# Hash bits as sign bits taken from PSUM, and sent by DMA instead of moved by VectorE

## The chip, the core and the metric

The kernel runs on one core of one Trainium2 chip. A core has five engines that run side by side, each with its own queue in order: TensorE (PE: matmul, with weight loads as PEld), VectorE (DVE), ScalarE (ACT), GpSimd (POOL) and SyncE (SP, which here only issues DMAs). Sixteen DMA engines move data between HBM and the on-chip memory (SBUF) and within SBUF. Matmul results land in PSUM, in tiles that pools share out. The metric is the device time of the whole kernel in microseconds.

## What is computed

Attention in which a query sees only keys of its own hash bucket, followed by a gated feed-forward block. Cut to what matters:

```python
# q, k, v: (4, 8, 768, 64); proj: (64, 6)
q_bits = (q @ proj > 0); k_bits = (k @ proj > 0)     # six bits each
mask = bucket(q_bits)[:, None] == bucket(k_bits)[None, :]
scores = where(mask, q @ k.T / 8, -1e9)
attn = softmax(scores); x = attn @ v                 # -> (3072, 512)
xn = x / sqrt(mean(x * x) + 1e-6) * rms_g
out = (silu(xn @ w_gate) * (xn @ w_val)) @ w_out
```

The kernel does not build the mask. It lays six more rows under the 64 rows of q and of k, one for each bit, each row +c or -c by the bit. The product of two matching bits is the same positive number, of two others its negative; where all six match the sum is 1536, and the exponential is taken with a bias of -192 after a scale of 1/8, so that any mismatch drops the weight to nearly nothing.

## The kernel before

**Tiling.** Four batches of eight heads; heads go in pairs (b, hp). A unit u is half of a batch's 768 queries (384) for all eight heads; there are eight units. Work is laid out in 192 steps. A step is a third of one head of one unit: two score matmuls of 128 keys by 384 queries (`scores`, L314) and one exponential over both (`probs`, L329). In each step the scores of the next step are issued first, then the exponential of this one, then a list of other work, `plan[t]`, filled by hand through `at(...)`. So each engine's order is fixed by the order in which the program issues; there is no scheduler behind it. The first two heads run for units 0 and 1 in turn, so the heads of pair 1 of batch 0 begin at step 12, of pair 2 at step 18, of pair 3 at step 24. The feed-forward block of a unit (`gate`, `value`, `project`) is spread over the steps of later units by `spread` (L692), which weighs pieces against a target per step; `inserts` holds pieces that are tied to a step (hash products, weight HASH, and sums of v, weight MEAN).

**Getting q and k.** A pair's q and k come from HBM as natural rows (batch 0 and the first two pairs of batch 1, `ONPE`) and are transposed on TensorE (`turn_pe`, L143); the PSUM result is copied into `qT` and `kT`, for batch 0's pairs 1 to 3 the k part by VectorE and the q part by ScalarE (L599 to L607). GpSimd casts them into the 16-bit tile `QK` (`cast_pool`). The other pairs come as 32 by 32 blocks and are transposed on VectorE (`turn_dve`). Values are cast by `v_prep`, on GpSimd but for pair 0.

**Hash bits.** `hash_direct` (L237), for ONPE pairs: small fp32 matmuls with proj give `d_ps` in PSUM, one group of 32 partitions for each of k and q of each head. VectorE makes signs (`signs`, L210: greater than 0, minus 0.5) into a tile `bits`. Then either VectorE copies six rows at a time to rows 64 to 69 of `QK` (`move`, L247: k scaled up to 512, q left at 0.5) or, for two pairs of batch 1, VectorE scales the whole tile by `own` and SP sends the rows by four DMAs (`send`, L257). In batch 0 all four pairs are moved by VectorE. `hash_one` (L268), for the ten other pairs: signs, then two multiplications by `sel` (`select`, L217) that blank the other head's bits, so that one DMA can write 12 rows for both heads; four DMAs per pair, and their score matmuls take 76 rows instead of 70.

**Queues.** SP issues in order the loads of q, k and v, the bits, and the stores of the output. In batch 0 its order is: loads of pair 3 of batch 0, values of pairs 2 and 3, then k, q and v of batch 1's pairs 0 and 1, then the block loads. Each of SP's DMAs uses one of eight semaphores and so waits for the landing of the eighth before it. GpSimd issues the feed-forward weights as casting DMAs: two halves of the gate weights (steps 3 and 7), two of the value weights (12 and 16), two of the output weights (39 and 42). All run on the same sixteen engines.

## Time and profile before

| | us |
|---|---|
| median of three runs | 341.23 (341.08 to 341.37) |
| profiled execution | 342.05 |
| its span | 340.3 |
| TensorE busy | 331.1 |
| VectorE busy | 249.0 |
| ScalarE busy | 226.7 |
| GpSimd busy | 152.9 |

Busy time is a sum over instructions; TensorE's matmuls overlap, so a busy TensorE is not one at its peak. A group of instructions is shown by its line in the code, engine, operation, result and source (partitions by elements), count, busy time, mean duration in ns, and idle time before it with what ended it. A stretch shows the busy time of each engine between two times. SP's rows are issues, and a row of several issues also holds the waits between them. When a DMA lands is told by the trace's DMA and semaphore records.

### The profile page before, as it was taken

Reading aid. Unit: us, or ns where it says so; the run is one execution under the profiler, and the core shown is the slowest. Engines: PE = TensorE matmul, PEld = TensorE weight load, DVE = VectorE, ACT = ScalarE, POOL = GpSimd, SP = SyncE. Lnnn points to the kernel's source line nnn. Section 1 sums busy time; section 2 is a strip of 40 time slices with the busy share of each in tenths; the row PEclk is TensorE's granted clock in tenths of the full one; section 3 lists DMA queues with packets and bytes.
Section 4 is the critical chain, followed back from the end, with each engine's and each line's share of the span. In section 5 each row is a group of like instructions: output and inputs, shape, how many; then the busy total and the mean of one; then the engine's idle time right before and its main releaser. Section 6 shows DMA issues by size and latency. Waiting matters only on the chain.

```text
span 340.3 us, 7757 instructions
## 1 busy us (share of the span) xinstructions
PE 331.1 (97%) x3004; PEld 198.0 (58%) x3004; DVE 249.0 (73%) x518; ACT 226.7 (67%) x331; POOL 152.9 (45%) x218
## 2 busy tenths in 40 slices
PE   8898999999999999999999999999999999999996
PEld 4465756655556555655656556555655656664554
DVE  3789996778889669977798758986796546674870
ACT  2889886666666767676667767776667767763322
POOL 4389939427553632746373523737280121112000
PEclk9999999999999999999999999999999999999999
DMA  7999965932728427251717017001100010001002
GB/s 222 291 213 272 236 119 91 173 103 46 165 49 158 91 94 144 35 115 64 133 55 139 7 68 157 24 3 41 64 7 4 1 64 33 0 2 64 31 0 92
DMA packets 79028, 31.20 MB, mean 92 GB/s; under 512 B 64928, under 2 KB 75024, under 8 KB 78992
## 3 DMA queue, kind: packets, MB, share of 16 engines
q1 hardware_dynamic: 75888, 25.73, 31.5%
q0 software_dynamic: 2656, 4.72, 8.0%
q8 instruction: 23, 0.38, 0.4%
q10 hardware_dynamic: 448, 0.27, 0.3%
q14 instruction: 13, 0.11, 0.1%
HBM read 28.32 MB, written 6.29 MB: 102 GB/s over the span
## 4 chain that ended last, share of the span: by engine, by line
PE 88%; DVE 7%; ACT 3%; issue 1%; DVEq 0%
PE g_ps L425 18%; PE v_ps L425 17%; PE y_ps L454 17%; PE s_ps L321 17%; PE o_ps L346 9%; PE d_ps L204 3%; PE x_ps L408 2%; DVE QK L251 2%; PE t_ps L150 2%; ACT psb L333 2%; PE d_ps L229 2%; DVE bits L212 1%; PE z_ps L525 1%; DVE a L442 1%; DVE kT L152 1%
## 5 line engine op out<-in xcount | busy, mean ns | idle before, releaser
L333 ACT ACTIVATE psb<-s_ps,ebias 128x768 f16<-128x768 f32 x192 | 168.3, 901 | 23.5 <-PE s_ps L321 22.7
L321 PE MATMUL s_ps<-QK 76*128 76x384 f16 (+1 forms) x384 | 93.8, 325 | 1.9 <-ACT psb L333 1.1
L433 ACT ACTIVATE t<-g_ps 128x384 f32<-128x384 f32 x96 | 47.2, 491 | 57.5 <-PE g_ps L425 57.3
L425 PE MATMUL g_ps<-xnT,wg 128*128 128x384 f16 x384 | 82.7, 325 | 0.4
L425 PE MATMUL v_ps<-xnT,wv 128*128 128x384 f16 x384 | 81.5, 325 | 0.7 <-DVE a L442 0.6
L442 DVE SCALAR_TENSOR_TENSOR a<-t,g_ps 128x384 f32<-128x384 f32 x96 | 52.8, 550 | 26.9 <-ACT t L433 25.3
L454 PE MATMUL y_ps<-wo,ht 128*128 128x512 f16 x276 | 68.0, 378 | 0.2 <-ACT ysb L466 0.2
L367 POOL TENSOR_TENSOR x<-otmp,rcp 128x384 f32<-128x384 f32 x31 | 25.7, 830 | 89.9 <-DVE rcp L365 89.4
L346 PEld LDWEIGHTS <-psb 128*128 128x128 f16 x1152 | 51.7, 97 | 19.6 <-issue 3.4
L443 DVE SCALAR_TENSOR_TENSOR ht<-a,v_ps 128x384 f16<-128x384 f32 x96 | 53.2, 554 | 11.1 <-PE v_ps L425 2.7
L346 PE MATMUL o_ps<-vl,psb 128*128 128x65 f16 x1152 | 56.4, 193 | 1.4 <-DVE otmp L360 1.4
L321 PEld LDWEIGHTS <-QK 76*128 76x128 f16 (+1 forms) x384 | 34.9, 98 | 35.1 <-issue 10.1
L425 PEld LDWEIGHTS <-wv 128*128 128x128 f16 x384 | 35.3, 97 | 23.3 <-issue 2.5
L425 PEld LDWEIGHTS <-wg 128*128 128x128 f16 x384 | 34.6, 97 | 21.7 <-issue 0.8
L454 PEld LDWEIGHTS <-ht 128*128 128x128 f16 x276 | 24.7, 97 | 22.9 <-issue 0.4
L196 POOL CAST QK<-kT 64x768 f16<-64x768 f32 x20 | 16.4, 822 | 23.2 <-DVE kT L183 11.8
L372 POOL TENSOR_TENSOR sq<-x 128x384 f32<-128x384 f32 x31 | 25.7, 828 | 2.4
L466 ACT COPY ysb<-y_ps 128x512 f32<-128x512 f32 x23 | 13.5, 587 | 18.5 <-PE y_ps L454 18.5
L196 POOL CAST QK<-qT 64x768 f16<-64x768 f32 x20 | 16.6, 830 | 18.7 <-DVE qT L183 17.4
L376 DVE TENSOR_REDUCE ssp<-sq 128x3 f32<-128x384 f32 x32 | 17.0, 530 | 10.2 <-POOL sq L372 10.1
L360 DVE TENSOR_TENSOR otmp<-o_ps,cvb 128x390 f32<-128x390 f32 x32 | 17.9, 559 | 6.1 <-PE o_ps L346 5.9
L414 DVE TENSOR_TENSOR xnT<-x_ps,gcol 128x512 f16<-128x512 f16 x22 | 14.5, 685 | 5.6 <-PE x_ps L408 5.6
(78 smaller groups left out, 282.5 us busy)
## 6 DMA issues: line engine op xcount, KB each, us to landing
vn<-in_v_dram SPq DMA_DIRECT2D x16, 384.0 KB
out_dram<-ysb SPq DMA_DIRECT2D x23, 256.0 KB
qL<-in_q_dram SPq DMA_DIRECT2D x40, 96.0 KB
kL<-in_k_dram SPq DMA_DIRECT2D x40, 96.0 KB
kn<-in_k_dram SPq DMA_DIRECT2D x5, 384.0 KB
qn<-in_q_dram SPq DMA_DIRECT2D x5, 384.0 KB
wg<-in_moe_w_gate_dram POOLq DMA_DIRECT2D x2, 768.0 KB, 11.3
wv<-in_moe_w_val_dram POOLq DMA_DIRECT2D x2, 768.0 KB, 10.2
```

Source lines behind the costliest of these rows:

```text
L196: nc.gpsimd.tensor_copy(QK[b, 2 * hp + hh, "h"][0:64, o : o + S], src[64 * hh : 64 * hh + 64, :])
L321: nc.tensor.matmul(ps[:, j, 0:HALF], QK[b, h, "h"][0:rows, S + jt * 128 : S + (jt + 1) * 128], QK[b, h, "h"][0:rows, half * HALF : (half + ...
L333: nc.scalar.activation(psb[u, h][:, 2 * ch : 2 * ch + 2, :], sps.pop((u, i))[:, :, 0:HALF], AF.Exp, bias=ebias, scale=ESCALE,)
L346: nc.tensor.matmul(o[:, c, hh, 0:65], psb[u, h][:, jt, c * 128 : (c + 1) * 128], vls[b % 2][:, h, 2 * (jt % 3) + jt // 3 if b in PARITY el ...
L360: nc.vector.tensor_add(tmp[:, :, :, 0:65], o[:, :, :, 0:65], cvb[b % 2][:, 2 * hp : 2 * hp + 2, 0:65].unsqueeze(1).to_broadcast([128, 3, 2 ...
L367: eng.tensor_mul(xd.rearrange("p c (h d) -> p c h d", h=2), tmp[:, :, :, 0:64], r.to_broadcast([128, 3, 2, 64]),)
L372: eng.tensor_mul(sq, xd, xd)
L425: nc.tensor.matmul(ps, w[:, kt, fs], xnT[u][:, kt, :], start=(kt == 0), stop=(kt == 3))
L433: nc.scalar.activation(t, fbank[u, ft, "g_ps"], AF.Tanh, scale=0.5)
L442: nc.vector.scalar_tensor_tensor(out=a, in0=t, scalar=1.0, in1=g, op0=ALU.add, op1=ALU.mult)
L443: nc.vector.scalar_tensor_tensor(out=ht[u][:, ft, :], in0=a, scalar=0.5, in1=vv, op0=ALU.mult, op1=ALU.mult)
L454: nc.tensor.matmul(y, ht[u][:, ft, c * 128 : (c + 1) * 128], wo[:, ft, :], start=(ft == 0), stop=(ft == NF - 1),)
```

## The change

*Bits.* proj is multiplied by -1 once, on GpSimd, so that the float sign bit of a hash product is set where the bit is 1. `signs` no longer compares: it reads the upper 16 bits of each fp32 value in PSUM, keeps the sign bit, and sets the bits 0x4C00, which makes the 16-bit float +16 or -16 for q and k alike. Bits thus have their full size at once, and `select`, `sel`, `own` and the scaled moves go.

*Batch 0, pair 0.* VectorE writes the signs of six rows straight from PSUM into `QK` (`direct`), eight instructions of 384 columns, in place of four sign instructions and eight moves.

*Batch 0, pairs 1 to 3.* The moves by VectorE (two steps and four steps after the hash) are replaced by `send_pair` one step after the hash: four DMAs on SP for each pair, head by head, k before q. The q copies from PSUM go from ScalarE to VectorE, and the value casts of pairs 1 to 3 from GpSimd to VectorE, one or two steps earlier.

*Batch 1, pairs 0 and 1.* The send stays where it was, without the scaling.

*The ten others.* `hash_one` sends each head's six rows by themselves: eight DMAs per pair in place of four, first head first; all score matmuls take 70 rows.

*spread.* A MEAN piece is now placed only when the step is full (or with what is left over), so it comes behind a feed-forward piece; a HASH piece as before.

On SP the order of batch 0 becomes: values of pairs 2 and 3, bits of pair 1, k, q and v of (1, 0), bits of pair 2, k, q and v of (1, 1), bits of pair 3, block loads.

```diff
-    KROWS = D + 12
-    KROWS0 = D + 6
+    KROWS = D + 6
...
-    def signs(bt, ps, c0, n):
+    def signs(dst, ps):
+        upper = ps.bitcast(U16).rearrange("p (c two) -> p c two", two=2)[:, :, 1]
         nc.vector.tensor_scalar(
-            out=bt[0:n, 1, c0 : c0 + HALF], in0=ps[0:n], scalar1=0.0, scalar2=0.5,
-            op0=ALU.is_gt, op1=ALU.subtract,
-        )
-    def select(bt, n, w):
-        for hh in range(2):
-            nc.vector.tensor_scalar_mul(
-                bt[0:n, hh, 0:w], bt[0:n, 1, 0:w], sel[0:n, hh : hh + 1]
-            )
+            out=dst.bitcast(U16), in0=upper, scalar1=SIGN, scalar2=BIT,
+            op0=ALU.bitwise_and, op1=ALU.bitwise_or,
+        )
...
-        where = [(which, hh) for which in "kq" for hh in heads]
+        where = [(which, hh) for hh in heads for which in "kq"]
...
-        def move(e, kinds="kq", n=1, only=heads):
...
+        def direct(which, e):
+            t = where.index((which, heads[0]))
+            o = (0 if which == "q" else S) + e * HALF
+            signs(
+                QK[b, 2 * hp + heads[0], "h"][D:KROWS, o : o + HALF],
+                pss[e][32 * t : 32 * t + 6],
+            )
         def send():
-            nc.vector.tensor_scalar_mul(bt[:, 0, :], bt[:, 1, :], own)
             for t, (which, hh) in enumerate(where):
                 o = 0 if which == "q" else S
                 nc.sync.dma_start(
-                    out=QK[b, 2 * hp + hh, "h"][64:KROWS0, o : o + S],
-                    in_=bt[32 * t : 32 * t + 6, 0, :],
+                    out=QK[b, 2 * hp + hh, "h"][D:KROWS, o : o + S],
+                    in_=bt[32 * t : 32 * t + 6, :],
                 )
...
-        select(bt, 128, HALF)
-        for t, which, half in where:
-            o = (0 if which == "q" else S) + half * HALF
-            nc.sync.dma_start(
-                out=QK[b, hp][64:KROWS, :, o : o + HALF],
-                in_=bt[32 * t : 32 * t + 12, :, 0:HALF],
-            )
+        for hh in range(2):
+            for t, which, half in where:
+                o = (0 if which == "q" else S) + half * HALF
+                p0 = 32 * t + 6 * hh
+                nc.sync.dma_start(
+                    out=QK[b, 2 * hp + hh, "h"][D:KROWS, o : o + HALF],
+                    in_=bt[p0 : p0 + 6, :],
+                )
...
+    nc.gpsimd.tensor_scalar_mul(pj, pj, -1.0)
...
-    sign(0)
-    move(0)
-    sign(1)
-    move(1, "k")
+    for which, e in (("k", 0), ("q", 0), ("k", 1)):
+        direct(which, e)
     scores(0, 0)
...
-        at(0, s0 + 2, turn_pe, 0, hp, 0, "q", nc.scalar.copy)
-        at(0, s0 + 3, turn_pe, 0, hp, 1, "q", nc.scalar.copy)
+        at(0, s0 + 2, turn_pe, 0, hp, 0, "q")
+        at(0, s0 + 3, turn_pe, 0, hp, 1, "q")
         at(0, s0 + 3, cast_pool, 0, hp, "q")
         at(0, s0 + 4, hash_pair, 0, hp)
-        at(0, s0 + 6, move_pair, 0, hp, 0)
-        at(0, s0 + 8, move_pair, 0, hp, 1)
+        at(0, s0 + 5, send_pair, 0, hp)
...
-    at(0, 9, v_prep, 0, 1)
-    at(0, 15, v_prep, 0, 2)
-    at(0, 21, v_prep, 0, 3)
+    at(0, 8, v_prep, 0, 1, nc.vector)
+    at(0, 13, v_prep, 0, 2, nc.vector)
+    at(0, 19, v_prep, 0, 3, nc.vector)
...
-                if extra and whole and t0 + s >= extra[0][0]:
+                full = done + weight // 2 > total * (s + 1) // n
+                if extra and whole and t0 + s >= extra[0][0] and (full or extra[0][1] > MEAN):
```

More of the change, by code (lines that the diff above doesn't have):

```diff
@@ L10 @@
 FP16 = mybir.dt.float16
+U16 = mybir.dt.uint16
 AF = mybir.ActivationFunctionType
@@ L22 @@
 HALF = 384
-BIT = 16.0
+SIGN, BIT = 0x8000, 0x4C00
 ESCALE = 1.0 / 8.0
@@ L67 @@
     pj = const.tile([128, 38], FP32, name="pj")
-    sel = const.tile([128, 2], FP32, name="sel")
-    own = const.tile([128, 1], FP32, name="own")
     ebias = const.tile([128, 1], FP32, name="ebias")
@@ L237, in hash_direct @@
     def hash_direct(b, hp, heads):
-        where = [(which, hh) for which in "kq" for hh in heads]
+        where = [(which, hh) for hh in heads for which in "kq"]
         pss = hash_pairs([turned(b, hp, which)[:, hh, :] for which, hh in where])
-        bt = spool.tile([128, 2, S], FP16, name="bits")
+        bt = spool.tile([128, S], FP16, name="bits")
         def sign(e):
-            signs(bt[:, :, e * HALF :], pss[e], 0, 32 * len(where))
-        def move(e, kinds="kq", n=1, only=heads):
-            for t, (which, hh) in enumerate(where):
-                if which in kinds and hh in only:
-                    o = (0 if which == "q" else S) + e * HALF
-                    nc.vector.tensor_scalar_mul(
-                        QK[b, 2 * hp + hh, "h"][64:KROWS0, o : o + n * HALF],
-                        bt[32 * t : 32 * t + 6, 1, e * HALF : (e + n) * HALF],
-                        4.0 * BIT * BIT if which == "k" else 1.0,
-                    )
+            signs(bt[:, e * HALF : (e + 1) * HALF], pss[e])
+        def direct(which, e):
[5 more added lines that the diff above has]
+            )
         def send():
-            nc.vector.tensor_scalar_mul(bt[:, 0, :], bt[:, 1, :], own)
             for t, (which, hh) in enumerate(where):
@@ L261, in send @@
                 nc.sync.dma_start(
-                    out=QK[b, 2 * hp + hh, "h"][64:KROWS0, o : o + S],
-                    in_=bt[32 * t : 32 * t + 6, 0, :],
+                    out=QK[b, 2 * hp + hh, "h"][D:KROWS, o : o + S],
+                    in_=bt[32 * t : 32 * t + 6, :],
                 )
-        return sign, move, send
+        return sign, direct, send
     def hash_one(b, hp):
@@ L274, in hash_one @@
         )
-        bt = spool.tile([128, 2, S], FP16, name="bits")
-        signs(bt, ps, 0, 128)
-        select(bt, 128, HALF)
-        for t, which, half in where:
-            o = (0 if which == "q" else S) + half * HALF
-            nc.sync.dma_start(
-                out=QK[b, hp][64:KROWS, :, o : o + HALF],
-                in_=bt[32 * t : 32 * t + 12, :, 0:HALF],
-            )
+        bt = spool.tile([128, HALF], FP16, name="bits")
+        signs(bt, ps)
+        for hh in range(2):
[6 more added lines that the diff above has]
+                )
     def v_prep(b, hp, eng=nc.gpsimd):
@@ L316, in scores @@
         h, ch = divmod(i, 3)
-        rows = KROWS0 if (b, h // 2) in ONPE else KROWS
         ps = scps.tile([128, 2, 512], FP32, name="s_ps")
@@ L322, in scores @@
                 ps[:, j, 0:HALF],
-                QK[b, h, "h"][0:rows, S + jt * 128 : S + (jt + 1) * 128],
-                QK[b, h, "h"][0:rows, half * HALF : (half + 1) * HALF],
+                QK[b, h, "h"][0:KROWS, S + jt * 128 : S + (jt + 1) * 128],
+                QK[b, h, "h"][0:KROWS, half * HALF : (half + 1) * HALF],
                 start=True, stop=True,
@@ L496 @@
     nc.sync.dma_start(out=gcol, in_=moe_rms_g.rearrange("(k p) -> p k", p=128))
-    nc.gpsimd.memset(sel, 0.0)
     make_identity(nc, ident)
-    for t in range(4):
-        p0 = 32 * t
-        nc.gpsimd.memset(sel[p0 : p0 + 12, :], 2.0 * BIT)
-        if t % 2 == 0:
-            nc.gpsimd.memset(sel[p0 : p0 + 6, 1:2], 0.0)
-            nc.gpsimd.memset(sel[p0 : p0 + 12, 0:1], 0.0)
-            nc.gpsimd.memset(sel[p0 : p0 + 6, 0:1], 2.0 * BIT)
-    nc.gpsimd.memset(own, 1.0)
-    for t in (0, 1):
-        nc.gpsimd.memset(own[32 * t : 32 * t + 6, :], 4.0 * BIT * BIT)
+    nc.gpsimd.tensor_scalar_mul(pj, pj, -1.0)
     nc.vector.memset(ebias, EBIAS)
@@ L551 @@
     idle(1)
-    sign, move, _ = hash_direct(0, 0, (0,))
+    _, direct, _ = hash_direct(0, 0, (0,))
     turn_pe(0, 0, 1, "q", nc.scalar.copy)
@@ L556 @@
         cast_part(0, 0, which, e, 1, 1)
-    sign(0)
-    move(0)
-    sign(1)
-    move(1, "k")
+    for which, e in (("k", 0), ("q", 0), ("k", 1)):
+        direct(which, e)
     scores(0, 0)
-    sign1, move1, _ = hash_direct(0, 0, (1,))
+    _, direct1, _ = hash_direct(0, 0, (1,))
     def second_head():
-        sign1(0)
-        move1(0)
-        sign1(1)
-        move1(1, "k")
-        move(1, "q")
-        move1(1, "q")
-    moves = {}
-    pair_signs = {}
+        for which, e in (("k", 0), ("q", 0), ("k", 1)):
+            direct1(which, e)
+        direct("q", 1)
+        direct1("q", 1)
+    pair_signs, sends = {}, {}
     def hash_only(b, hp):
-        pair_signs[b, hp], *moves[b, hp] = hash_direct(b, hp, (0, 1))
+        pair_signs[b, hp], _, sends[b, hp] = hash_direct(b, hp, (0, 1))
     def hash_signs(b, hp):
@@ L586, in hash_pair @@
         hash_signs(b, hp)
-    def move_pair(b, hp, hh):
-        moves[b, hp][0](0, n=2, only=(hh,))
     def send_pair(b, hp):
-        moves[b, hp][1]()
+        sends[b, hp]()
     at(0, 0, second_head)
@@ L705, in spread @@
                     continue
-                if done + weight // 2 > total * (s + 1) // n:
+                if full:
                     break
```

## The prediction

> **What bounds the kernel now.** I read the busy table first, then the waits of TensorE, then busy time by stretch, because the change acts mostly in batch 0 (to 48 us).

> ```profile
> PE 331.1 (97%) x3004; PEld 198.0 (58%) x3004; DVE 249.0 (73%) x518; ACT 226.7 (67%) x331; POOL 152.9 (45%) x218
> 20.00:25.00 5.00, 4.52 (x62) 2.91 (x61) 4.52 (x10) 4.49 (x8) 3.97 (x6) 1.00 1.03 172
> 25.00:30.00 5.00, 4.37 (x62) 2.83 (x62) 4.84 (x8) 4.70 (x7) 4.76 (x7) 1.00 1.07 254
> 30.00:35.00 5.00, 4.37 (x57) 3.12 (x56) 4.81 (x11) 4.33 (x7) 4.86 (x6) 1.00 1.08 282
> 35.00:40.00 5.00, 5.00 (x71) 3.52 (x67) 4.52 (x10) 4.04 (x5) 4.63 (x8) 1.00 1.12 260
> 60.00:300.00 240.00, 238.77 (x2157) 141.94 (x2155) 181.19 (x376) 167.45 (x241) 107.15 (x138) 1.00 0.34 72
> ```

> The stretches give PE, PEld, DVE, ACT, POOL, then clock, DMA share and GB/s. From 60 to 300 us TensorE is busy 99.5%: what other engines save there is worth nothing, and a delay suffered earlier is kept to the end. From 20 to 40 us all engines are near full, VectorE at 90 to 97%, and so are the 16 DMA engines (share 1.03 to 1.12; 0.34 later). So a cut of VectorE work can pay there, and a transfer put there meets the worst traffic. Next the queue that is to carry the bits (start, time, what), and the loads beside it:

> ```profile
> 15.84 0.42 SPq L94 DMA_DIRECT2D kn<-in_k_dram  x1
> 19.59 0.37 SPq L94 DMA_DIRECT2D qn<-in_q_dram  x1
> 21.17 0.37 SPq L103 DMA_DIRECT2D vn<-in_v_dram  x1
> 25.62 0.37 SPq L94 DMA_DIRECT2D kn<-in_k_dram  x1
> 26.08 0.42 SPq L94 DMA_DIRECT2D qn<-in_q_dram  x1
> 27.37 0.37 SPq L103 DMA_DIRECT2D vn<-in_v_dram  x1
> ...
> 48.77 5.94 SPq L261 DMA_DIRECT2D QK<-bits  x8
> ...
> wg<-in_moe_w_gate_dram POOLq DMA_DIRECT2D x2, 768.0 KB, 11.3
> ```

> The DMA records behind these rows tell when each landed on all its engines. The gate weights were issued at 16.86 and 19.50; their packets filled the engines from 18.9. The load issued at 19.59 had no packet started before 23.73 and landed at 30.0; those of 21.17, 25.62, 26.08 and 27.37 landed at 35.0, 38.1, 39.7 and 43.9 (14 of 16 engines: 31.9, 36.4, 37.8, 39.0). The eight bits transfers (batch 1, the very form that the change adds) took 1.84 us from issue to landing on quiet engines (four of them, 50.47 to 52.31 the first). The first, behind a value load on this queue that landed at 51.61, landed at 51.64: the queue keeps its order. The last two, issued at 53.35 and 54.05 as an output-weight load began, took 4.0 and 5.4 us.

> **The change part by part.** Durations are from these groups:

> ```profile
> L251 DVE TENSOR_SCALAR QK<-bits 6x768 f16<-6x768 f16 x12 | 8.2, 683 | 0.3
> L251 DVE TENSOR_SCALAR QK<-bits 6x384 f16<-6x384 f16 x8 | 1.9, 250 | 0.2
> L212 DVE TENSOR_SCALAR bits<-d_ps 64x384 f16<-64x384 f32 x4 | 2.2, 550 | 1.6 <-PE d_ps L229 1.5
> L219 DVE TENSOR_SCALAR bits<-bits,sel 128x384 f16<-128x384 f16 x20 | 11.6, 579 | 0.7
> L152 ACT COPY qT<-t_ps 128x384 f32<-128x384 f32 x7 | 3.4, 481 | 2.4 <-PE t_ps L150 2.3
> L258 DVE TENSOR_SCALAR bits<-bits,own 128x768 f16<-128x768 f16 x2 | 1.4, 680 | 0.0
> ```

> *Start-up, pair 0.* Four signs and eight moves (4 x 0.55 + 8 x 0.25 = 4.2 us of VectorE) become eight signs from PSUM straight into QK. No row shows that form: 0.25 (the small move) to 0.55 (the PSUM source) each, so 2.0 to 4.4; I take 0.55, the source being the same. Until the first scores it is 2 x 0.55 against 0.55 + 2 x 0.27: nothing, and after that 0.2 us at most. Nothing.

> *Scaling proj by -1 on GpSimd* waits for both proj loads (landed 5.4 by the records), then some 0.25 us, as the 128x4 scale has (244 ns). The hash product reads it at 7.34, so 1.6 us spare. Six memsets behind it move some 2.5 us later, the first cast from 6.07 to about 6.6; its reader is the scores at 10.7. Eleven memsets on sel and three on own go. Nothing.

> *Pairs 1 to 3 of batch 0.* VectorE loses 12 moves (8.2 us), gains six q copies at 0.55 (3.3) and three value casts at 0.56 (1.7): -3.2 us. ScalarE loses 6 x 0.48, GpSimd 3 x 0.86. Per pair (six steps) VectorE falls from 6.3 to 5.3 us (two copies 1.1, signs 1.0, moves 2.7, mean 0.3, output step 1.3 before; four copies 2.2 and a cast 0.56 for the moves after); TensorE needs some 5.2 (six scores 1.95, hash 0.8, attention 1.1, transposes 1.3). So a pair that waits for nothing takes 5.4 to 5.5 us instead of 6.3 and 5.9. This is the gain.

> *The price: twelve bits transfers on SP.* Each pair's four are issued at 0.66 us (659 to 862) after its signs, in the order k, q of the first head, k, q of the second. The scores of steps 12, 18 and 24 (first head of pair 1, 2, 3) wait for the first two. They ran at 21.95, 28.25 and 34.18. Behind those scores on TensorE stand all its later work, so ScalarE and VectorE dry up too.

> Pair 1: signs end at about 18.4 as before (17.35 + 1.02). k goes at 18.4, q at 19.07. On quiet engines q would land at 20.9, before step 12 wants it (21.4). But gate packets start at 18.9, and what arrived at a quiet ring after them stood still until 23.73. Bounds 20.9 to 28.9 (one transfer per 16 weight packets, as the last two output-weight cases suggest); nearest is the load issued at 19.59, so 24.4. Step 12: +2.45.

> Pair 2: signs end at 26.9. The three loads formerly issued from 15.84 to 21.17 now come behind pair 1's bits, at 21.0 to 22.2, all ahead of these bits: 768 packets of 1536 bytes. Without weights in the way the queue moved 210 packets per us, with them 52. At best: gate weights until 29, 260 packets by then, the rest in 2.4 us: 32. At worst both value-weight loads come between: 39.7. The third load in line had 11 of 16 engines by 33.6 before; I take 33.5. Without a wait step 18 would stand at 24.4 + 5.5 = 29.9, so the wait is 3.6 and step 18 comes at +5.25.

> Pair 3: signs end at 36, k and q issued by 37.4, landing 39 at the earliest; ahead are three more loads, whose last had 14 engines at 39.0 and all at 43.9. A bits transfer has six data packets and six closing writes in the records, so it need not wait for the slowest engine. I take 41. Unhindered step 24 would be at 33.5 + 5.4 = 38.9. Step 24: 41.0 against 34.18, +6.8.

> Steps 24 to 38 took 13.5 us (34.18 to 47.68); two moves (1.13) and one own-scale (0.94) go from a VectorE that was full, with TensorE's floor near 11.7: -0.8. Sum: +6.0 at step 38.

> [...]

> *After 48 us.* hash_one loses 20 selections (11.6 us of VectorE) and sends 8 transfers instead of 4: 8 x 0.66 = 5.3 us on SP against 4 x 0.85. Its narrowest case is the pair signed at 93.03 and wanted at 99.56; the first half-heads now leave at 93.7 and land near 96. The stores behind on SP have slack: SP waited 103 us for ScalarE's copies. Score rows 76 to 70 change nothing (326 and 325 ns). The mean's product goes behind a piece of its slot instead of ahead: same count. All hidden under TensorE's 99.5%. Nothing. Batch 1's own-scale goes, its send was held by block loads, not by it.

> Sum: 342.05 of the profiled execution + 6.0 = 348.05; the median shown is 0.82 below that execution, so 347.2.

> **The rivals.**
> "In time": the bits land in 1.84 us everywhere, as four of eight did. Then only the gain is left: step 12 -0.55, two pairs -0.8 and -0.5, later -0.8, about -2.6: 338.6. It needs q of pair 1 down by 21.4; the stop to 23.73 and the landing at 51.64 behind a load speak against it. It decides where landings take under 2.3 us.
> "Overtaking": bits wait for the running weight packets but not for loads ahead. Step 12 +2.45, step 18 at 29.9, step 24 at 35.3 (+1.1), end +0.3: 341.5.
> "Turns": pair 1's q waits for a second gate load (28.9), pairs 2 and 3 for both value-weight loads (39.7, then 46). Step 24 +11.8, end +11.0: 352.2. For it: two transfers 0.7 us apart landed 2 us apart under weights. Against it: from 23.7 to 29 the load's and the weights' packets ran one to one.

> **How the numbers follow.** Forecast 0.70 with its own range 343.9 (pair 2 at 32, pair 3 not held: 34.18 + 3.4, less 0.7) to 351; "turns" 0.12; "in time" 0.10; "overtaking" 0.08, half of it within 0.2% (about what a measurement of this kernel can tell from no change), a quarter each side. Faster 0.12, same 0.04, slower 0.84. The range 342.5 to 352.3 leaves out "in time", "overtaking" and the tails.

> **What would show it.** Right: score matmuls wait for a bits DMA three times, with step 12 near 24.4, step 18 near 33.5, step 24 near 41; VectorE idle in these stretches where it was 97% busy; from 60 us on the same stretches, shifted. Wrong: no DMA among TensorE's releasers, or a shift at 48 us that is not in the end; or a wait after 60 us for bits or for SP's later loads.

## The result and the profile after

The changed kernel takes 350.88 us (median of four, 348.41 to 353.21) against 341.3 us before in the same job: ratio 1.0277, 95% interval 1.0201 to 1.0354. It is slower, by 9.6 us in the medians. The profiled execution is the fastest of the four: 348.41 us, span 346.5, against 342.05 and 340.3 before, so the traces differ by 6.4 us in time and 6.2 us in span.

From the page of the changed kernel: busy time by engine, the granted clock in 40 slices of 8.7 us, and the chain that ended last by engine:

```profile
PE 331.5 (96%) x3004; PEld 199.0 (57%) x3004; DVE 233.4 (67%) x489; ACT 224.3 (65%) x325; POOL 148.4 (43%) x202
...
PEclk9999699999999999999999999999999999999999
...
PE 85%; DMA 4%; DVE 3%; ACT 1%; issue 1%; SPq 0%; DVEq 0%
```

VectorE lost 15.6 us of work and TensorE kept its own, yet DMA now has 4% of the chain. One slice, from 34.7 us, shows a clock of 0.6. Busy time by stretch, in the columns of the prediction:

```profile
15.00:20.00 5.00, 4.51 (x74) 3.12 (x73) 3.50 (x9) 3.17 (x5) 4.66 (x6) 1.00 0.74 171
20.00:25.00 5.00, 2.33 (x33) 1.56 (x35) 2.50 (x6) 2.16 (x3) 4.73 (x6) 1.00 1.04 203
25.00:30.00 5.00, 4.94 (x75) 3.67 (x74) 3.71 (x9) 4.34 (x6) 2.31 (x4) 1.00 1.06 300
30.00:35.00 5.00, 0.19 (x7) 0.06 (x3) 0.82 (x2) 0.65 (x1) 4.72 (x7) 0.84 1.08 254
35.00:40.00 5.00, 4.85 (x42) 2.35 (x43) 1.67 (x4) 1.81 (x3) 0.16 (x1) 0.50 1.09 300
60.00:300.00 240.00, 239.69 (x2162) 142.89 (x2160) 171.78 (x358) 167.93 (x242) 114.40 (x148) 1.00 0.35 73
```

For half of the stretch from 20 to 25 us, and nearly all of that from 30 to 35 us, TensorE, VectorE and ScalarE stand still together, while the DMA engines stay full (1.04 and 1.08). From 35 to 40 us TensorE is busy but at half clock, with 42 matmuls where there were 71. From 60 us on TensorE is as busy as before. What stopped TensorE, from its waits (sum, times, longest):

```profile
PE s_ps L311 <- DMA QK<-bits: 7.6, 2, 5.0
```

And the links of the chain, in order of time, that are transfers of bits (issue, time to landing):

```profile
19.51 4.88 DMA QK<-bits
...
27.73 7.28 DMA QK<-bits
```

These are the q rows of the first heads of pairs 1 and 2. SP's queue shows when they went out and what lay between (a row of four issues takes 2.84 to 2.99 us):

```profile
18.60 2.99 SPq L251 DMA_DIRECT2D QK<-bits  x4
21.64 0.45 SPq L94 DMA_DIRECT2D kn<-in_k_dram  x1
22.19 0.40 SPq L94 DMA_DIRECT2D qn<-in_q_dram  x1
22.69 0.42 SPq L103 DMA_DIRECT2D vn<-in_v_dram  x1
26.98 2.84 SPq L251 DMA_DIRECT2D QK<-bits  x4
29.92 0.39 SPq L94 DMA_DIRECT2D kn<-in_k_dram  x1
30.41 0.40 SPq L94 DMA_DIRECT2D qn<-in_q_dram  x1
30.91 0.42 SPq L103 DMA_DIRECT2D vn<-in_v_dram  x1
38.58 2.84 SPq L251 DMA_DIRECT2D QK<-bits  x4
```

By the DMA records pair 1's k and q landed at 23.85 and 24.38, pair 2's at 34.47 and 35.02, pair 3's at 42.31 and 42.70. The score matmuls of the steps began at:

| step | before | predicted | after | shift |
|---|---|---|---|---|
| 12 (pair 1) | 21.95 | 24.4 | 24.52 | +2.6 |
| 18 (pair 2) | 28.25 | 33.5 | 35.15 | +6.9 |
| 24 (pair 3) | 34.18 | 41.0 | 42.84 | +8.7 |
| 38 | 47.68 | 53.7 | 55.86 | +8.2 |
| 101 | | +6.0 | | +7.8 |
| 118 | | +6.0 | | +6.6 |
| 191 (last) | 301.18 | 307.2 | 307.65 | +6.5 |

So there are three things to explain: the two waits (the larger part), the half clock behind the second, and a gain of 1.7 us after step 100 that was not forecast.

### The profile page after: what moved, and what is told of

The parts are those of the page before. It is cut to its first block, busy times and chain, and to the rows that moved or that the text cites. A ratio compares the mean times of both kernels' runs of the same rounds, so it can differ in the third digit from the quotient of the medians.

```text
span 346.5 us, 7807 instructions
## 1 busy us (share of the span) xinstructions
PE 331.5 (96%) x3004; PEld 199.0 (57%) x3004; DVE 233.4 (67%) x489; ACT 224.3 (65%) x325; POOL 148.4 (43%) x202
## 4 chain that ended last, share of the span: by engine, by line
PE 85%; DMA 4%; DVE 3%; ACT 1%; issue 1%; SPq 0%; DVEq 0%
PE v_ps L415 18%; PE g_ps L415 17%; PE y_ps L444 17%; PE s_ps L311 16%; PE o_ps L336 9%; DMA QK<-bits 4%; PE d_ps L202 3%; PE x_ps L398 2%; PE d_ps L222 1%; PE y_ps L463 1%; PE t_ps L148 1%; ACT psb L323 1%; DVE bits L211 1%; PE m_ps L296 1%; DVE a L432 0%
## 5 line engine op out<-in xcount | busy, mean ns | idle before, releaser
L323 ACT ACTIVATE psb<-s_ps,ebias 128x768 f16<-128x768 f32 x192 | 167.8, 899 | 34.4 <-PE s_ps L311 33.4
L311 PE MATMUL s_ps<-QK 70*128 70x384 f16 x384 | 94.7, 328 | 9.4 <-DMA QK<-bits 7.6
L336 PEld LDWEIGHTS <-psb 128*128 128x128 f16 x1152 | 52.4, 97 | 19.0 <-issue 4.3
L433 DVE SCALAR_TENSOR_TENSOR ht<-a,v_ps 128x384 f16<-128x384 f32 x96 | 53.2, 554 | 11.3 <-PE v_ps L415 3.1
L311 PEld LDWEIGHTS <-QK 70*128 70x128 f16 x384 | 34.9, 98 | 42.0 <-issue 11.6
L415 PEld LDWEIGHTS <-wv 128*128 128x128 f16 x384 | 35.2, 97 | 22.6 <-issue 1.8
L415 PEld LDWEIGHTS <-wg 128*128 128x128 f16 x384 | 34.7, 97 | 21.2 <-DVE xnT L404 0.6
L456 ACT COPY ysb<-y_ps 128x512 f32<-128x512 f32 x23 | 13.5, 585 | 18.6 <-PE y_ps L444 18.6
L211 DVE TENSOR_SCALAR bits<-d_ps 128x384 uint16<-128x384 uint16 x20 | 10.7, 553 | 14.2 <-PE d_ps L222 11.5
## 6 DMA issues: line engine op xcount, KB each, us to landing
wg<-in_moe_w_gate_dram POOLq DMA_DIRECT2D x2, 768.0 KB, 8.5
wv<-in_moe_w_val_dram POOLq DMA_DIRECT2D x2, 768.0 KB, 9.8
```

The costliest lines, as they stand in the source:

```text
L311: nc.tensor.matmul(ps[:, j, 0:HALF], QK[b, h, "h"][0:KROWS, S + jt * 128 : S + (jt + 1) * 128], QK[b, h, "h"][0:KROWS, half * HALF : (half ...
L323: nc.scalar.activation(psb[u, h][:, 2 * ch : 2 * ch + 2, :], sps.pop((u, i))[:, :, 0:HALF], AF.Exp, bias=ebias, scale=ESCALE,)
L336: nc.tensor.matmul(o[:, c, hh, 0:65], psb[u, h][:, jt, c * 128 : (c + 1) * 128], vls[b % 2][:, h, 2 * (jt % 3) + jt // 3 if b in PARITY el ...
L415: nc.tensor.matmul(ps, w[:, kt, fs], xnT[u][:, kt, :], start=(kt == 0), stop=(kt == 3))
L433: nc.vector.scalar_tensor_tensor(out=ht[u][:, ft, :], in0=a, scalar=0.5, in1=vv, op0=ALU.mult, op1=ALU.mult)
```

## The experiments

The theory after the result: the sent bits land late because their transfers run beside weight loads and behind SP's own loads; everything else in the change is worth little. The rivals: another part of the change costs (the work moved to VectorE, the scaling of proj), or the loss is in the half clock.

### The send undone

`e1_moves_back` keeps the change but for batch 0's pairs 1 to 3, which go back to moves by VectorE, q copies on ScalarE and value casts on GpSimd.

```diff
-        at(0, s0 + 2, turn_pe, 0, hp, 0, "q")
-        at(0, s0 + 3, turn_pe, 0, hp, 1, "q")
+        at(0, s0 + 2, turn_pe, 0, hp, 0, "q", nc.scalar.copy)
+        at(0, s0 + 3, turn_pe, 0, hp, 1, "q", nc.scalar.copy)
...
-        at(0, s0 + 5, send_pair, 0, hp)
+        at(0, s0 + 6, lambda hp=hp: moves[0, hp](0))   # tensor_copy, 6 x 768, k and q
+        at(0, s0 + 8, lambda hp=hp: moves[0, hp](1))
...
-    at(0, 8, v_prep, 0, 1, nc.vector)   # and 13, 19 for pairs 2, 3
+    at(0, 9, v_prep, 0, 1)              # and 15, 21
```

> The changed kernel with batch 0's pairs 1 to 3 put back as before: bits copied into QK by VectorE two and four steps after the hash, q copies on ScalarE, value casts on GpSimd. What stays of the change: full-size signs, the direct signs of pair 0, hash_one without selections and with eight transfers, the MEAN rule. Theory (the twelve early transfers are the loss): TensorE waits for no bits DMA, scores of steps 12, 18, 24 within 0.5 us of before (21.95, 28.25, 34.18), and the 1.7 us that the changed kernel gains after step 96 stays: about 339.6. Rival (the loss is in what stays, such as one more queue load on SP or the order of the pieces): still above 345. Second rival (the gain after step 96 came from the shift, not from the selections): 341.3.

Measured: 340.50 us (339.91 to 340.82, seven runs) against 341.57, ratio 0.9968 (0.9957 to 0.9979). Steps 12, 18 and 24 at 21.96, 28.31 and 34.22. In the stretches of this run all three engines are full again:

```profile
20.00:25.00 5.00, 4.17 (x61) 2.63 (x60) 4.57 (x10) 4.27 (x8) 3.98 (x6) 1.00 1.07 227
25.00:30.00 5.00, 4.33 (x62) 2.79 (x62) 4.84 (x8) 4.70 (x7) 4.76 (x7) 1.00 1.07 284
30.00:35.00 5.00, 4.38 (x55) 3.14 (x54) 4.81 (x11) 4.29 (x7) 4.86 (x6) 1.00 1.09 287
```

So the loss is in these lines, and what stays of the change is a gain of 1.1 us. Against before, its shift is -0.1 at step 71, -0.5 at 101, -1.3 at 113, -1.6 at 118: a gain late, as in the changed kernel.

### The send alone

`e2_send_alone` is the kernel before with only the send put in, its scaling by `own` on VectorE included.

```diff
-        at(0, s0 + 6, move_pair, 0, hp, 0)
-        at(0, s0 + 8, move_pair, 0, hp, 1)
+        at(0, s0 + 5, send_pair, 0, hp)
...
-            for t, (which, hh) in enumerate(where):
+            for t, (which, hh) in sorted(enumerate(where), key=lambda e: (e[1][1], e[0])):
```

> The kernel before, with one thing changed: batch 0's pairs 1 to 3 send their bits by four DMAs on SP one step after the hash, with the own-scale on VectorE ahead, in place of the moves. q copies and value casts stay on ScalarE and GpSimd. Theory: the waits come with the transfers alone, step 12 near 25, step 18 near 35, TensorE's clock drops after the second wait as in the changed kernel, end 7 to 12 us above before, 348 to 353. Rival (the q copies and casts moved to VectorE make the bits late): steps 12 and 18 within 1 us of before, about 341.

Measured: 353.67 us (353.0 and 354.34), ratio 1.0359 (1.0333 to 1.0385). Steps 12, 18, 24 at 24.86, 34.62 and 44.0. Its waits of TensorE:

```profile
PE s_ps L321 <- DMA QK<-bits: 9.1, 3, 4.2
```

Three waits, of 4.18, 2.69 and 2.25 us. There is no late gain: the shift of 11.2 us at step 28 stays. The send alone costs more than the whole change, and 0.7 us more than the top of the expected band.

### The work moved to VectorE, with and without the send

`e9_moves_on_dve` takes the first run and leaves q copies and value casts on VectorE; `e10_copies_back` takes the change and puts them back on ScalarE and GpSimd.

```diff
 e9, against e1
-        at(0, s0 + 2, turn_pe, 0, hp, 0, "q", nc.scalar.copy)   # and s0 + 3
+        at(0, s0 + 2, turn_pe, 0, hp, 0, "q")
-    at(0, 9, v_prep, 0, 1)              # and 15, 21
+    at(0, 8, v_prep, 0, 1, nc.vector)   # and 13, 19
 e10, against the change: the same lines the other way
```

> The change with all of it kept but the send: six rows moved by VectorE at s0+6 and s0+8, q copies and value casts of pairs 1 to 3 on VectorE. Per pair VectorE then has the prediction's 6.3 us (before) plus two q copies (1.1) and a value cast (0.56), about 7.9 us, where the pair of the kernel before took 5.9 to 6.3. My theory, that VectorE sets the pace of batch 0 while all pairs are moved by it: each of the three pairs lasts 1 to 1.6 us longer than with the copies on ScalarE and the casts on GpSimd, a shift of +3 to +5 us at step 38 against the run that moves and copies as before (340.5), so 343.5 to 345.5. Rival, that VectorE has room there and only the chain from the hash to the moved bits counts: within 0.7 us of 340.5.

> The change with the send kept, but q copies on ScalarE and value casts on GpSimd as before. If the landing of the bits sets the steps 12, 18 and 24, VectorE idles beside it and the place of these 5 us of work is worth little: within 1 us of the change (350.9), steps 12, 18 and 24 within 0.5 us of 24.5, 35.2 and 42.8. Rival, that the copies on VectorE buy time (5.5 us a pair, as predicted): 1.5 to 2.5 us slower than the change, which would also account for the 353.7 of the send put alone into the kernel before.

| | copies on ScalarE, casts on GpSimd | both on VectorE |
|---|---|---|
| bits moved by VectorE | 340.50 (e1) | 344.79 (e9; 343.79 to 345.94) |
| bits sent by DMA | 348.22 (e10; 344.91 to 349.48) | 350.88 (the change) |

Kernels before: 341.3 for the change, 341.57 for e1, 341.89 for e9 and e10. The ratio of e9 is 1.0090 (1.0064 to 1.0117), of e10 1.0158 (1.0097 to 1.0219). With moves, the extra VectorE work costs 4.3 us, within the band that was expected. Its trace shows where, on VectorE and then on TensorE:

```profile
22.36 0.53 DVE L150 COPY qT<-t_ps 128x384 f32<-128x384 f32 x1
22.92 1.52 DVE L252 COPY QK<-bits 6x768 f16<-6x768 f16 x2
24.47 0.56 DVE L150 COPY qT<-t_ps 128x384 f32<-128x384 f32 x1
```

```profile
25.09 1.39 PE L222 MATMUL d_ps<-qT,pj 64*32 64x384 f32 x4 [1.26 <-DVE qT L150]
```

The second half of a q waits behind the moves of the pair before it, and the hash products wait for it. With sends the place of the copies is within what these runs can separate (the intervals of e10 and of the change overlap). The expected band of 1 us was missed by the median, on the side away from the rival, and e10's steps 12, 18 and 24 began at 24.23, 33.71 and 42.22, the second 1.4 us sooner than in the change: copies on VectorE bought no time.

### What the transfers wait for

`e3_weights_late` moves the weight loads out of the stretch; `e5_loads_late` moves SP's loads of batch 1 behind the bits.

```diff
 e3
-        at(0, 3 + 4 * i, load_w, wg, moe_w_gate, 2 * i, 2)
-        at(0, 12 + 4 * i, load_w, wv, moe_w_val, 2 * i, 2)
+        at(0, 19 + i, load_w, wg, moe_w_gate, 2 * i, 2)
+        at(0, 21 + i, load_w, wv, moe_w_val, 2 * i, 2)
 e5 (first entry of each list: the loads of k, q and v)
-    for hp, ts in ((0, (8, 22, ...)), (1, (12, 27, ...))):
+    for hp, ts in ((0, (13, 22, ...)), (1, (19, 27, ...))):
```

> The changed kernel with the four gate and value weight loads issued at steps 19 to 22 instead of 3, 7, 12 and 16, so that none runs beside the first two sends. Theory by the weights: the bits of pair 1 land 1.9 us after issue (about 21), those of pair 2 too, since the loads ahead run at 210 packets per us and are down by 26; steps 12 and 18 without a wait, near 21.5 and 27. Rival (the loads ahead on SP's queue alone make the bits late): step 18 still waits 3 us or more. Either way the weights now land 8 to 10 us later than before, so a new wait for them is likely at the first gate product, at about 47 us, of 2 to 8 us; the end tells nothing by itself.

Measured: 341.43 us (340.17 to 343.69, seven runs), ratio 0.9987 (0.9970 to 1.0004): level with before. Its waits of TensorE for bits and its stretches of pair 1 and pair 2:

```profile
PE s_ps L311 <- DMA QK<-bits: 1.5, 1, 1.5
```

```profile
21.39:27.74 6.35, 5.98 (x82) 3.98 (x79) 4.98 (x11) 5.28 (x7) 4.72 (x6) 1.00 0.60 195
27.74:33.79 6.05, 5.67 (x79) 3.35 (x75) 4.36 (x10) 4.68 (x7) 5.77 (x8) 1.00 0.69 201
```

Steps 12 and 18 are on time (21.39, 27.74). Pair 3 met the postponed weights: five rows of its k, issued at 30.51, had landed by 33.70, the first weight packet started at 34.0, and the sixth row landed at 34.97. The profiled execution lost some 3.4 us more to the clock behind that wait (343.69; the six others, at a granted clock of 1.0, took 340.17 to 341.99). A later wait for the weights themselves, which the expectation held likely, did not show.

> The changed kernel with the loads of batch 1's first two pairs issued one step behind the sends of pair 2 and pair 3 (steps 13 and 19 in place of 8 and 12), so that no load stands ahead of pair 2's bits on SP's queue; the weight loads stay. Theory (order of the queue and weights together): pair 1 as in the changed kernel (step 12 near 24.5), but pair 2's bits, issued at 27, wait only for the running gate packets and land by 30 to 31 instead of 34.5 to 35, so step 18 comes at about 30.5. Rival (the weights alone do it, whatever is ahead on SP): step 18 again near 35. Behind it k of (1, 0) now arrives late, so that a new wait is likely at its transposes in step 22, and the end says little.

Measured: 346.26 us (346.12 and 346.41), ratio 1.0135 (1.0116 to 1.0155). Waits for bits in this run:

```profile
PE s_ps L311 <- DMA QK<-bits: 4.3, 3, 2.8
```

The first wait stays (step 12 at +2.9), the second has shrunk to 0.26 us, and a third of 1.24 us remains. Step 18 came at 33.43, between the theory's 30.5 and the rival's 35: after the first wait TensorE ran at half clock from 24.27 to 31.09, so the bits went out only at 28.26 and 28.97, and they landed at 33.10 and 33.30. This run's times of steps thus decide little; its landings count. From the DMA records of all these runs, issue to landing of the k rows of a first head:

| beside a weight load | behind SP's loads | us |
|---|---|---|
| no | no | 1.98 (e3 pair 1; the three transfers behind it 1.84 to 1.85) |
| no | yes | 1.88 (e5 pair 3), 2.84 (e3 pair 2) |
| yes | no | 4.8 to 5.5 (pair 1 of the change, e2, e4, e5 and e10; e5 pair 2) |
| yes | yes | 3.7 to 7.5 (pair 2: e2 and e4 4.9, e10 6.3, the change 7.5; pair 3: 5.2, 5.8, 4.7, 3.7) |

So a weight load in progress is the main cost, some 3 us a transfer in most cases (1.8 us in the least); loads ahead on its own queue, still on their way, add between nothing and 1.0 us in quiet, and under weights between nothing and 2.7 us, varying from one execution to the next.

### The half clock

`e4_fill_pe` adds matmuls of zeros, whose result nothing reads, where TensorE waited.

```diff
+    at(0, 10, idle, 12, bank)
+    at(0, 16, idle, 22, bank)
```

> The changed kernel with products of zeros that nobody reads, 12 of them ahead of the scores of step 12 and 22 ahead of those of step 18, so that TensorE is busy for 2.6 and 4.8 us of its two waits. They add work that the waits hide. Theory (half of the clock after the 5 us wait is due to TensorE's idle time): granted clock 1.0 all through, steps 12 and 18 as in the changed kernel (24.5, 35.2), steps 18 to 24 in 5.5 to 6 us instead of 7.7, so about 1.5 to 2 us off the profiled 346.5 and more off the median of 350.9, with runs closer together than 348 to 353. Rival (the low clock has another cause, such as power or the DMA traffic): clock again 0.5 between 35 and 40 us and no gain.

Measured: 350.92 us (350.55 to 351.6), ratio 1.0281 (1.0264 to 1.0297): the time of the change. TensorE around the second wait and the third:

```profile
29.77 4.91 PE L505 MATMUL z_ps<-zeros 128*128 128x512 f16 x22
34.52 0.44 PE L336 MATMUL o_ps<-vl,psb 128*128 128x65 f16 x9
34.80 0.49 PE L311 MATMUL s_ps<-QK 70*128 70x384 f16 x2
...
43.45 0.48 PE L311 MATMUL s_ps<-QK 70*128 70x384 f16 x2 [2.99 <-DMA QK<-bits]
```

The clock stayed at 1.00 in every stretch of 1 us from 20 to 44 us, and the work of steps 18 to 24 took 5.65 us until TensorE stood still (34.80 to 40.45; with step 24 at the end, 7.69 in the change). But the gain did not come: pair 3's bits, issued 1.35 us earlier than in the change (37.23 against 38.58), landed at 43.02 and 43.31, 0.6 to 0.7 us later, and TensorE waited 3.0 us for them. The half clock of the changed kernel thus hid the third wait that the prediction has; taking it away uncovers that wait and ends at the same place. A limit of this run: the zeros themselves held step 18 until 34.80, though its bits had landed at 32.55, so it does not say what this execution would have done with no half clock and no filling.

### The late gain

`e6_mean_old` and `e7_select_kept` each undo, on top of the first run, one of the two things that differ after step 100. The second multiplies the bits twice by a column of ones, for the time of the selections.

```diff
 e6
-                if extra and whole and t0 + s >= extra[0][0] and (full or extra[0][1] > MEAN):
+                if extra and whole and t0 + s >= extra[0][0]:
 e7, in hash_one
+        for _ in range(2):
+            nc.vector.tensor_scalar_mul(bt, bt, one)
```

> The kernel of the first experiment (moves back) with the placing rule of the MEAN pieces as before. It tells where the 1.7 us come from that are gained between steps 96 and 170. If from the selections that VectorE no longer makes: the gains at steps 101, 113, 118 and 164 stay (some 1.6 us in the profile). If from the MEAN rule: they go.

> The kernel of the first experiment with two multiplications by one put behind the signs in each hash_one, as long as the two selections were. If the selections made the late gain: it goes again, steps from 120 on within 0.3 us of before. If the MEAN rule made it: it stays.

Measured, one execution each: 341.61 and 341.66 us. Against before the first run gains 0.36 us at step 101, 0.8 at 113, 0.35 at 118 and 0.12 at 164. With the old MEAN rule only the 0.8 at 113 is left. With the multiplications kept, the gains at 101, 118 and 164 are left, the one at 113 is gone and 0.3 is lost at 104. Just before step 113 a value product waits for VectorE; this is the group in the waits of the kernel before (the wait ends at 176.6 us), and then in those of e7 (it ends at 176.7):

```profile
PE v_ps L425 <- DVE a L442: 0.6, 1, 0.6
```

```profile
PE v_ps L431 <- DVE a L448: 0.8, 2, 0.6
```

In the change and in e1 the group is 0.2 us, once. So the late gain is two halves of about 0.8 us: VectorE without selections is in time for a value product, and a MEAN product behind its feed-forward piece lets that piece go first.

### The scaling of proj

`e8_no_negation` is the first run without it; the sign bit then marks the other value, in q and k alike, and the products are the same.

```diff
-    nc.gpsimd.tensor_scalar_mul(pj, pj, -1.0)
```

> The kernel of the first experiment without the scaling of proj by -1: the sign bit then marks the other value of each bit, for q and k alike, so the product of two bits is the same. GpSimd no longer stands between proj's landing and the first hash product. Theory (the scaling sits on the start-up path, where TensorE waited 1.2 us for it in the profile of the first experiment): the wait falls to 0.3 us, steps from 0 on come 0.3 to 0.9 us earlier, and the median is 339.7 to 340.3 against 340.5. Rival (the landing of proj itself sets it, scaling 0.34 us at most): 340.2 to 340.5.

Measured: 340.29 us (339.79 to 340.54, five runs), ratio 0.9956 (0.9942 to 0.9970). The first hash product no longer waits for GpSimd, but 0.4 us for VectorE's copy of k. Against e1's 0.9968 (0.9957 to 0.9979) the 0.2 us of difference can't be told from none. Its median is the lowest of all versions run, level with e1's, and 1.3 us below the kernel before.

## Why the prediction came out as it did

The direction and the mechanism were right, and in the profiled execution the size: +6.0 us forecast, +6.4 measured. Part of that is luck. Two errors cancel, and the profiled execution was the fastest of the four; in the medians +6.0 us was forecast (347.2) and +9.6 measured (350.88). By its own steps:

- *Start-up, pair 0: nothing.* Right: the new sign from PSUM takes the 0.55 us that was taken, and the first scores start at 9.39 instead of 9.49.

```profile
L211 DVE TENSOR_SCALAR QK<-d_ps x8: 542/548/552, 8.2 to 12.9; 6x384 uint16<-6x384 uint16 x8
```

- *Scaling proj: nothing, with 1.6 us spare.* The price held, by e8, though the scaling took 0.34 us and not 0.25. In the change it ended at 5.97, 1.2 us before the first hash product (7.21; 7.34 before). In e1 the second load of proj landed only at 6.35 (5.44 in the change); the scaling ran from 6.54 to 6.88, and the first hash product waited 1.2 us for it, to 6.93, as e1's waits of TensorE show. So the spare time hangs on when proj lands. The product still starts no later than before.

```profile
PE d_ps L222 <- POOL pj L501: 1.2, 1, 1.2
```

- *The gain, 5.4 to 5.5 us a pair.* Wrong, and the one step whose reasoning failed. Where pairs waited for no bits (e3) they took 6.35 and 6.05 us against 6.30 and 5.93 before, though VectorE had fallen from 92 and 97% to 78 and 72%. These are the same two stretches before, and the work of pair 2 in e4, which took 5.65 us:

```profile
21.95:28.25 6.30, 5.67 (x80) 3.81 (x77) 5.82 (x12) 5.83 (x9) 6.02 (x8) 1.00 1.06 216
28.25:34.18 5.93, 5.30 (x80) 3.15 (x77) 5.73 (x11) 5.66 (x8) 5.66 (x7) 1.00 1.08 286
34.80:40.45 5.65, 5.27 (x79) 3.22 (x75) 3.21 (x8) 4.52 (x6) 1.24 (x3) 1.00 1.08 298
```

  The last of them shows that TensorE's own need, put at 5.2 us, was about right. What failed is that a pair was taken to last as long as the busiest engine's sum. In e3 TensorE and VectorE wait for each other in turn, over pieces that the change itself put on VectorE:

```profile
21.19 0.99 DVE L150 COPY qT<-t_ps 128x384 f32<-128x384 f32 x2
22.23 0.84 PE L222 MATMUL d_ps<-qT,pj 64*32 64x384 f32 x4
24.53 0.56 DVE L150 COPY kT<-t_ps 128x384 f32<-128x384 f32 x1 [0.42 <-PE t_ps L148]
25.01 1.01 DVE L280 CAST vl<-vn 128x768 f16<-128x768 f32 x1
27.47 0.43 PE L336 MATMUL o_ps<-vl,psb 128*128 128x65 f16 x9 [0.30 <-DVE otmp L350]
```

  The second half of the hash products starts as VectorE's q copies end (22.18), and by the chains of the two traces the 16 products take 1.19 us where they took 0.94 before. On VectorE a value cast takes 1.01 us, where 0.56 was put down, and the output step that the value products at 27.47 wait for (`otmp`) comes behind it and three more pieces. Matmuls of a run overlap (48 of these products, of 495 ns each, fill 6.0 us of the kernel before), so the first of these waits does not show as idle time, and the 5.98 us of a busy TensorE are more than its need. Which of these pieces would have to go for the gain to come was not tried. That VectorE's order counts is also what e9 shows: loading it further, with the bits moved, costs 4.3 us.
- *Pair 1's landing, 24.4, step 12 at +2.45.* Right: 24.38, step 12 at 24.52.
- *Pair 2's landing, step 18 at 33.5.* Right in kind, 1.65 us short: 35.02 and 35.15. The same transfer landed at 32.55 to 34.48 in e2, e4 and e10 (issued at 27.51 to 29.40, against 27.73 here), so 33.5 is in the middle and the profiled execution was at the late end.
- *Pair 3, a third wait, step 24 at 41.0.* The term for 18 to 24, 5.4 us, was mis-sized: it took 7.69, because TensorE ran at half clock, which the prediction did not have. The wait did not show for that reason: the bits, issued later than forecast (q at 39.33 against 37.4), had landed at 42.70, and step 24 began at 42.84. e2 and e4, which reach the end of pair 2's work sooner, both have it.
- *Steps 24 to 38, -0.8.* Measured -0.5 (13.02 against 13.50).
- *After 48 us, nothing.* Wrong by -1.7, as e6 and e7 show. "Busy 99.5%" was read as no wait left; the waits left are the 0.6 us for VectorE and products that stand in a poor order, which a busy share does not show. Without this error the forecast would have been worse: the shift at step 38 was +8.2, not +6.0.
- *The median, 0.8 below the execution's sum.* Wrong: the median is 2.5 above the profiled execution, mostly because the other three lost more to the clock (last section).

Of the rivals, "in time" is what e3 made nearly true at pairs 1 and 2 (landings of 1.84 to 2.84 us, no wait), and it gave 341.4 rather than 338.6, for want of the gain. "Turns" fell: that each of SP's transfers lets a whole weight load pass was the author's estimate, and no run shows it; pair 1's q landed at 24.38, not 28.9, pair 2's at 35.02, not 39.7, and pair 3's at 42.70, not 46; of the two slowest executions, which came near its 352.2, 353.21 goes with its half clock (below); 351.85 lost no more to the clock than 349.92 did, and what held it up is not known, as only the fastest execution left a trace. "Overtaking" holds only in part: e2 and e4 saw pair 2's bits pass as quickly behind loads as without them, the change itself did not.

## What to carry to other kernels

Price a transfer at the traffic it will meet: these six-row copies land in 1.84 us in quiet and in 3.7 to 7.5 us beside a weight load, and putting the weights elsewhere, or the copy back on an engine, was worth 9 to 10 us here. Relieving an engine that is 92 to 97% busy in a stretch bought nothing in e3 (VectorE at 78 and 72%, and pairs of 6.35 and 6.05 us against 6.30 and 5.93): before such a gain is counted, read what each step waits for last there, and what the work that is moved will stand in front of. And where a new wait may stop TensorE, count what the clock may take behind it: here most waits of 1.5 to 5.0 us were followed by 3.41 or 6.83 us at 0.5, by an estimate up to 1.7 us lost in each 3.41 (half of it).

## What was not expected of the hardware

| | window before (us) | TensorE busy in it | at half clock |
|---|---|---|---|
| the change | 30.0 to 33.4 | 0.06 | 6.83 |
| e2 | 21.6, 31.8, 42.1 (starts) | 0.04, 0.21, 0.43 | 3.41 each |
| e3 | 31.3 to 34.8 | 0.62 | 6.83 |
| e4 | 40.9 to 44.3 | 0.25 | 3.41 |
| e5 | 20.9 to 24.3 | 0.34 | 6.83 |
| e9 | 21.8 to 25.2 | 0.50 | 3.41 |
| e10 | 21.9, 32.1, 38.9 (starts) | 0.31, 0.53, 0.43 | 3.41 each |

At full clock no window between 13 and 52 us under 0.55 was without a fall; windows at 0.60, 0.62 (the change) and 0.64 (e5) had none, against the one at 0.62 in e3. So idle times of 1.5 to 2.8 us, or several that add up, were enough here when they filled about half of a window, and once with 0.38 of it (e3); by an estimate, half of 3.41, they cost up to 1.7 us a window. For a window that itself ran at half clock more was needed: TensorE busy 0.48, 0.83 and 0.85 of it (the change, e5, e3) was followed by another at half clock, and 1.00 by full clock. Within one execution the stretches begin whole windows apart (10.2 us, three times 3.41, between those of e2; 10.2 and 6.8 in e10), but from one execution to the next at other places: at 33.4, 25.0, 34.8, 44.3 and 24.3 us in the change, e2, e3, e4 and e5, which leaves 2.7, 1.1, 0.6, 3.3 and 0.4 on windows of 3.41. That the same wait therefore falls now into one window and now into two is the author's estimate. The clock lost makes most of the spread of the changed kernel: 3.5 us in the fastest execution and 8.4 in the slowest, which is 4.8 us longer. Span times the share of the clock that was not granted tells how many windows each execution lost (0.01 of 346.5 us is 3.5 us lost, two windows of 1.7):

| | windows at half clock | us |
|---|---|---|
| the change | 2, 3, 3, 5 | 348.41, 349.92, 351.85, 353.21 |
| e10 | 1, 1, 3, 3 | 344.91, 347.08, 349.35, 349.48 |
| before (of e1's measurement), e1 | 0 | 341.10 to 342.75, 339.91 to 340.82 |

The 349.92 and 351.85 us of the change, at three windows each, and the 344.91 and 347.08 us of e10, at one, show that something else adds some 2 us; what, no trace here tells.

The gap of 1.49 us in e3 was followed by 6.83 us at 0.5, which began inside it. What the busy share must reach exactly was not tried.
